# A wider list schedule for the tail of a fused attention, gated-expert and cosine MLP kernel

## The chip, the cores and the metric

The kernel runs on one core of a Trainium2 chip. A core has five engines that take their instructions in program order, each from its own queue, and meet at semaphores: TensorE (PE in the profile, with its weight loads as PEld), VectorE (DVE), ScalarE (ACT), GpSimd (POOL) and SyncE (SP, which here issues most of the DMAs). The metric is the device time of one launch in microseconds (us).

## The reference

```python
def _attn_ref(q, k, v):                    # (2, 8, 576, 64)
    scores = scale * np.matmul(q, k.transpose(0, 1, 3, 2))
    mask = (rel >= 0) & (rel < 64)
    attn = softmax(np.where(mask, scores, -1e9))
    return np.matmul(attn, v)

def _moe_ref(x, domain_probs, w1, w2):     # x (1152, 512), 4 experts 512 -> 1024 -> 512
    p = domain_probs / (domain_probs.sum(-1, keepdims=True) + 1e-09)
    for e in range(E):
        h = np.maximum(x @ w1[e], 0.0)
        out += p[:, e:e + 1] * (h @ w2[e])

def _moe2_ref(x, w_in, w_out):             # 512 -> 2048 -> 512
    h = x @ w_in
    g = h * np.cos(h)
    return g @ w_out
```

The three run one behind the other on the same 1152 tokens.

## The kernel before

Every product of float32 numbers is made as three matmuls of rounded parts (high by high, low by high, high by low), so each tile that enters a product exists as a high part (`xhi`, `thi`, `whi`, `w7hi`, `hh`), which ACT makes, and a low part (`xlo`, `tlo`, `wlo`, `w7lo`, `hl`), which DVE or POOL makes as the difference. PE adds the three products up in a PSUM bank.

The program has two parts. The **hand-written part** holds the attention and the first steps of the gated experts, in the order of the string `ORDER`. The gated experts are cut into eight halves e of an expert; a step (e, g, f) treats one group g of token columns with one block f of hidden columns. Its A step (L431 to L433, or L628 in the scheduled part) makes the hidden block, L444 its high and L447 its low part; its B step (L469) adds the block's share into the PSUM accumulators `pb_acc` of the group, and behind the last f one `add_expert` for each accumulator (L478 for the first half, L480 for the others, on DVE) adds it, times the gate, to `acc` in SBUF and so frees the bank. There are four such accumulator banks. The line `for what, s in seq[:T2 + 1]` emits the steps that are written by hand; with T2 = 30 the last of them are B(1,1,0), B(1,1,1) and A(0,2,0).

All that follows is the **scheduled part**: the code makes a list of jobs (`job`, `either` for a job that DVE or POOL may take), each with an engine, a duration from a formula, what it depends on, and the PSUM banks or buffers that it takes or uses (`Slots`, `Hold`). It holds the rest of the first two halves (L628, L469), the seven-product units of the other halves (`a_unit`, `b_unit`), and the cosine MLP. In `a_unit` PE makes products `y` and `seed` from `xhi`, `thi` and the weights `w7` (L1037); ACT copies a `seed` (L1051) or a product `p` (L1055) back into PSUM or SBUF, DVE adds (L1068 `y`, L1077 `c`), and the finished sum goes through ACT and DVE into `hh` and `hl` (L444 and L1130 for the experts; for the cosine MLP `kk` through L1146, L1151, L1157, L1158 and L1163, then `hh` L1166 and `hl` L1172). `b_unit` adds them up in PSUM (L1231 `pb_acc`), and L480 or L1256 takes them out. Beside it run: sums of weights (`sums` L850) with their parts (L869, L874, L913, L918), sums of token columns (`tsum` L944, L953, parts L966, L969), the change of the last weights from 64-bit words (`m`, `x`: L737 to L770 on DVE and POOL), and, between the experts and the cosine MLP, `turn` and `token_sums`, which transpose `acc` on PE (`psx` L1303) and make new `xhi` (L1318), `xlo` (L1328) and `tsum` (L1371 to L1403) of it.

The planner `plan` plays the jobs through. A job's due time `late` is worked out backwards from the PE jobs in their order. PE takes its jobs in the order of `pe_list`, with leave to look eight ahead; another engine that is free takes, of the jobs that are ready, the one with the earliest due time. `plan` runs three times, each time with the starts of the last one, and the instructions of all engines are then written out in the order of the planned starts. On the chip nothing is reordered any more: an instruction whose data is late holds up what stands behind it on its engine.

One detail matters for the adds: `std_bs` makes the `Hold` on the accumulators only at f = 0. For the half (1,1), whose f = 0 step is hand-written, `std_finish` finds no `Hold`, so the planner does not know that the adds of (1,1) free the banks that the B step of (0,2) wants.

Of the kernel before, what the change touches and what calls it, by code (L numbers as in the profile page):

```python
# [26 lines left out]
def tile_window_attention_moe_cosglu(  # L27
# [20 lines left out]
    NE, DM, FF = w1.shape  # L48
# [3 lines left out]
    NFC = FE // P  # L52
    SPL = FF // FE
# [477 lines left out]

    T2 = 2 * SPL * 2 * NFC - 2
    for what, s in seq[:T2 + 1]:
# [43 lines left out]
    def dve_ns(n):  # L577
        return 77 + 1.01 * n
# [69 lines left out]
    def std_bs(s):  # L648
        e, g, f = steps[s]
        no = GS[g] // P  # L650
        deps = [std_ready.get(s), std_b.get(s - 1)]
        if f == 0:
            std_hold[e, g] = [Hold(accs) for _ in range(no)]
        holds = std_hold.get((e, g), ())

        def matmuls():
            emit_b(s)

        b = std_b[s] = pe(
            no * 3 * mm_ns(DM), matmuls, deps,  # L660
            new=holds if f == 0 else (), use=holds if f else (),
        )
        return b
# [3 lines left out]
    def std_finish(e, g, b):  # L667
        k, c = SG[g], GC[g] // P
        for i in range(GS[g] // P):
            def add(i=i):  # L670
                p = gate_p[:, G0[g] // P + i, e // SPL:e // SPL + 1]
                add_expert(e, acc[k][:, c + i, :], std_pss[e, g][i], p)
            hold = std_hold.get((e, g))
            std_done[k, c + i] = job(
                "DVE", dve_ns(DM), add, [b], use=[hold[i]] if hold else ()
            )

# [789 lines left out]
    POOLMAX = 9999  # L1467
    QUIET = 1
    SOON = 60000.0
    place = {j: i for i, j in enumerate(pe_list)}  # L1470
# [24 lines left out]

    def plan(starts):
        line = list(pe_list)
# [43 lines left out]
        engines = ["PE", "ACT", "DVE", "POOL", "SP", None]  # L1541
        waiting = {e: [] for e in engines}

        def arrive(j):
# [10 lines left out]
        while events:  # L1555
# [59 lines left out]
        return began  # L1615

    rank = {j: i for i, j in enumerate(topo)}
# [59 lines left out]
```

## Time and profile before

| | |
|---|---|
| median of three runs | 638.83 us (637.6 to 639.07) |
| the profiled execution, its own time | 639.75 us |
| its span, from the first to the last instruction | 637.8 us |
| outside the span | 1.95 us |
| PE busy | 622.8 us, 98% of the span |
| DVE busy | 470.6 us, 74% |
| ACT busy | 335.2 us, 53% |
| POOL busy | 156.9 us, 25% |

The time of the profiled execution is 0.92 us above the median. A stretch's busy times tell which engine is full there, the granted clock which of PE's two levels it had (1.00 is 2.4 GHz, 0.50 is 1.2 GHz), and the timeline which instruction PE waited for: a row's bracket holds the idle time ahead of the instruction and the instruction that ended it.

### The profile page before, as it was taken

What the parts mean: (1) busy time and instruction counts of PE and PEld (TensorE: products, weight loads), DVE (VectorE), ACT (ScalarE), POOL (GpSimd) and SP (SyncE); (2) the same over time, 40 slices, a digit from 0 to 9 for tenths busy, and PEclk for the clock granted to TensorE, in tenths of its full rate; (3) what the DMA queues carried; (4) which work ended last, traced back from release to release, by engine and by line L of the source; (5) the groups of instructions that cost most, each with busy time, mean ns of one, the idle gap of its engine ahead of it and who ended that gap; (6) DMA issues with size and microseconds to landing.
All of it is one profiled execution on the core that took longest, in us unless ns stands there. A gap on an engine that the chain in (4) does not pass through costs nothing.

```text
span 637.8 us, 10837 instructions
## 1 busy us (share of the span) xinstructions
PE 622.8 (98%) x4019; PEld 553.2 (87%) x4019; DVE 470.6 (74%) x990; ACT 335.2 (53%) x840; POOL 156.9 (25%) x169
## 2 busy tenths in 40 slices
PE   8999999899999999999999999999899999999997
PEld 7878898688888989989999988998799988999896
DVE  5858536544999799889789699787857677676664
ACT  5957313232345244335344244457878978777653
POOL 6985101230022110223333220212114124121000
PEclk9999999899999999999999999999899999999999
DMA  9943200260055444444446645204001202000022
GB/s 299 294 149 105 69 1 29 71 197 1 1 166 163 135 131 133 166 133 166 137 130 208 186 132 166 68 0 133 2 1 58 76 7 93 2 1 1 1 67 83
DMA packets 37254, 63.10 MB, mean 99 GB/s; under 512 B 2761, under 2 KB 18633, under 8 KB 37202
## 3 DMA queue, kind: packets, MB, share of 16 engines
q1 hardware_dynamic: 36386, 61.63, 30.8%
q10 hardware_dynamic: 816, 0.79, 0.4%
q8 instruction: 31, 0.51, 0.4%
q14 instruction: 21, 0.17, 0.1%
HBM read 51.66 MB, written 10.75 MB: 98 GB/s over the span
## 4 chain that ended last, share of the span: by engine, by line
PE 85%; DVE 7%; ACT 3%; DMA 2%; issue 1%; POOL 1%; DVEq 0%; SPq 0%; POOLq 0%
PE pb_acc L1231 37%; PE y L1037 19%; PE seed L1037 14%; PE pb_acc L469 7%; PE ph L628 2%; ACT e L284 1%; PE ph L431 1%; PE ph L433 1%; PE ph L432 1%; DMA raw<-in_moe_w_dram 1%; PE psv L324 1%; DVE acc L480 1%; PE pss L260 1%; PE pst L309 1%; DVE tsum L944 1%
## 5 line engine op out<-in xcount | busy, mean ns | idle before, releaser
L1231 PE MATMUL pb_acc<-whi,hh 128*128 128x512 f32 x360 | 142.1, 395 | 2.3 <-DVE xlo L1328 2.3
L1231 PE MATMUL pb_acc<-wlo,hh 128*128 128x512 f32 x360 | 142.1, 395 | 0.0
L1231 PE MATMUL pb_acc<-whi,hl 128*128 128x512 f32 x360 | 140.8, 391 | 0.0
L1037 PE MATMUL y<-xhi,w7hi 128*128 128x256 f32 (+1 forms) x320 | 95.3, 298 | 0.8 <-DVE hl L1172 0.5
L1037 PE MATMUL y<-xhi,w7lo 128*128 128x256 f32 (+1 forms) x320 | 94.7, 296 | 0.0
L1037 PE MATMUL y<-xlo,w7hi 128*128 128x256 f32 (+1 forms) x320 | 94.7, 296 | 0.0
L1231 PEld LDWEIGHTS pb_acc<-whi,hl 128*128 128x128 f32 x360 | 67.9, 189 | 15.5
L1231 PEld LDWEIGHTS pb_acc<-whi,hh 128*128 128x128 f32 x360 | 67.9, 189 | 12.0 <-issue 2.5
L1231 PEld LDWEIGHTS pb_acc<-wlo,hh 128*128 128x128 f32 x360 | 67.9, 189 | 8.7
L1037 PE MATMUL seed<-thi,w7hi 128*128 128x320 f32 (+1 forms) x240 | 71.4, 298 | 2.0 <-DVE y L1068 1.0
L1037 PE MATMUL seed<-thi,w7lo 128*128 128x320 f32 (+1 forms) x240 | 70.7, 295 | 0.0
L1037 PE MATMUL seed<-tlo,w7hi 128*128 128x320 f32 (+1 forms) x240 | 70.6, 294 | 0.0
L1037 PEld LDWEIGHTS y<-xhi,w7hi 128*128 128x128 f32 x320 | 60.6, 189 | 3.1 <-DVE hl L1172 0.7
L1037 PEld LDWEIGHTS y<-xlo,w7hi 128*128 128x128 f32 x320 | 60.6, 189 | 1.8
L1037 PEld LDWEIGHTS y<-xhi,w7lo 128*128 128x128 f32 x320 | 60.4, 189 | 0.0
L874 POOL TENSOR_TENSOR w7lo<-raw,w7hi 128x256 fp32r<-128x256 f32 (+1 forms) x21 | 17.9, 856 | 139.0 <-DVE sums L850 50.3
L1037 PEld LDWEIGHTS seed<-thi,w7hi 128*128 128x128 f32 x240 | 45.1, 188 | 7.5 <-DVE y L1068 1.2
L480 DVE SCALAR_TENSOR_TENSOR acc<-pb_acc,gate_p,acc 128x512 f32<-128x512 f32 x63 | 46.1, 744 | 6.3 <-PE pb_acc L1231 6.3
L1037 PEld LDWEIGHTS seed<-tlo,w7hi 128*128 128x128 f32 x240 | 45.1, 188 | 3.8
L444 ACT ACTIVATE hh<-y 128x320 fp32r<-128x320 f32 (+1 forms) x48 | 19.5, 407 | 50.2 <-PE y L1037 50.1
L918 POOL TENSOR_TENSOR wlo<-raw,whi 128x512 fp32r<-128x512 f32 x20 | 26.4, 1328 | 78.5 <-ACT whi L913 43.8
L1037 PEld LDWEIGHTS seed<-thi,w7lo 128*128 128x128 f32 x240 | 45.1, 188 | 0.0
(141 smaller groups left out, 1323.7 us busy)
## 6 DMA issues: line engine op xcount, KB each, us to landing
raw<-in_moe_w_dram SPq DMA_DIRECT2D x32, 512.0 KB, 5.2
raw<-in_moe_w_in_dram SPq DMA_DIRECT2D x16, 512.0 KB, 4.3
w<-x SPq DMA_DIRECT2D x32, 256.0 KB, 4.7
raw<-in_moe_w_out_dram SPq DMA_DIRECT2D x16, 512.0 KB, 4.4
raw<-w SPq DMA_DIRECT2D x16, 512.0 KB, 3.4
vr<-in_v_dram SPq DMA_DIRECT2D x16, 256.0 KB, 4.3
out_dram<-acc SPq DMA_DIRECT2D x18, 128.0 KB, 1.7
qraw<-in_q_dram SPq DMA_DIRECT2D x16, 128.0 KB, 3.7
```

The costliest lines, as they stand in the source:

```text
L260: nc.tensor.matmul(out=out[h][W * c:W * (c + 1), p], lhsT=qts[c][rows, p, :], rhs=kts[c][rows, p, :], start=True, stop=True,)
L284: nc.scalar.activation(out=e[:, p], in_=s[:, p], func=AF.Exp, bias=nm[:, p:p + 1], scale=1.0, accum_out=sm[:, p:p + 1],)
L309: nc.tensor.transpose(out=ps[:, p], in_=pn[:, p], identity=ident)
L324: nc.tensor.matmul(out=pv[W * h:W * (h + 1), p, W * c:W * (c + 1)], lhsT=vts[c][:, P * p + W * h:P * p + W * (h + 1)], rhs=pts[h][:, p, W ...
L444: nc.scalar.activation(out=hh, in_=ps, func=AF.Relu)
L469: nc.tensor.matmul(out=ps, lhsT=a, rhs=b, start=first and m == 0, stop=last and m == 2)
L480: nc.vector.scalar_tensor_tensor(out=a, in0=ps, scalar=p, in1=a, op0=ALU.mult, op1=ALU.add)
L628: nc.tensor.matmul(out=ps, lhsT=a[:, d, cs], rhs=b[:, d, :], start=d == 0 and m == 0, stop=d == KD - 1 and m == 2,)
L874: return engine.tensor_tensor(out=operand(w_lo[x], i), in0=part(i), in1=operand(w_hi[x], i).bitcast(F32), op=ALU.subtract,)
L918: return engine.tensor_tensor(out=w_lo[x][:, i], in0=box["t"][:, i], in1=w_hi[x][:, i].bitcast(F32), op=ALU.subtract,)
L1037: nc.tensor.matmul(out=ps, lhsT=a[:, WI[i], d, :], rhs=b[:, d, :], start=start and d == 0 and m == 0, stop=d == 1 and m == 2, skip_group_c ...
L1231: nc.tensor.matmul(out=ps, lhsT=a, rhs=b[:, fo, :], start=first and fo == 0 and m == 0, stop=last and fo == 1 and m == 2,)
```

## The change

Three steps of the gated experts, B(1,1,0), B(1,1,1) and A(0,2,0), go from the hand-written part to the scheduler (T2 is lower by three). Holds on the accumulators are made for every group, so that the adds of (1,1) count as what frees the banks. In `plan` a job that takes several slots starts only when so many are free; DVE, ACT and POOL leave a job that is ready if a more urgent one is to arrive before it would end (`waits_better`); and due times get a random addition of up to 0, 300 or 1000 ns. In place of three passes there are 120 plans; each is played back in its written order with random delays (`rehearse`), and the best one is written out.

```diff
-    T2 = 2 * SPL * 2 * NFC - 2
+    T2 = 2 * SPL * 2 * NFC - 5
...
         deps = [std_ready.get(s), std_b.get(s - 1)]
-        if f == 0:
+        begun = (e, g) in std_hold
+        if not begun:
             std_hold[e, g] = [Hold(accs) for _ in range(no)]
-        holds = std_hold.get((e, g), ())
+        holds = std_hold[e, g]
+        if f and not begun:
+            job(None, 0.0, lambda: None, new=holds)
...
-            hold = std_hold.get((e, g))
-            std_done[k, c + i] = job(
-                "DVE", dve_ns(DM), add, [b], use=[hold[i]] if hold else ()
-            )
+            std_done[k, c + i] = job("DVE", dve_ns(DM), add, [b], use=[std_hold[e, g][i]])
...
+    PLANS = 120
...
-    def plan(starts):
+    def plan(starts, jitter):
...
+        open_ = {j: len(j.deps) for j in jobs}
+        coming = {e: {} for e in engines}
+        soon = {j: 0.0 for j in jobs}
+
+        def waits_better(j, e, ns):
+            end = now + ns
+            return any(
+                now < at < end and u.late < end and j.late > at + u.ns
+                for x in (("DVE",) if e == "POOL" else (e,)) for u, at in coming[x].items()
+                if e == x or u.port
+            )
...
-                            free[h.slots] > (e == "SP" or e == "PE" and j is not todo[0])
+                            free[h.slots] >= len(j.new) + (e == "SP" or e == "PE" and j is not todo[0])
                             for h in j.new
...
+                    if e in ("DVE", "ACT", "POOL"):
+                        ns = {"DVE": dve_ns, "POOL": pool_ns}.get(e)
+                        ok = [j for j in ok if not waits_better(j, e, ns(j.size) if j.size else j.ns)]
                     if not ok:
                         break
-                    j = ok[0] if e == "PE" else min(ok, key=lambda j: (j.late, j.n))
+                    j = ok[0] if e == "PE" else min(ok, key=lambda j: (j.late + jitter[j], j.n))
...
+                    coming[e].pop(j, None)
+                    for o in j.out:
+                        open_[o] -= 1
+                        soon[o] = max(soon[o], now + j.ns + gap(j, o))
+                        if not open_[o] and not o.size and o.eng != "PE":
+                            coming[o.eng][o] = soon[o]
...
+    def rehearse(starts, seed):
+
+        draw = random.Random(seed)
+        line = sorted(jobs, key=lambda j: (starts[j], rank[j]))
...
+                for o in j.out:
+                    left[o] -= 1
+                    late = draw.uniform(-SPARE, 0.0) if j.eng == "SP" else 0.0
+                    at[o] = max(at[o], now + gap(j, o) + late)
...
+                    ns = j.ns * (1.0 if e == "PE" else 1.0 + abs(draw.gauss(0.0, 0.02)))
+                    busy[e] = now + ns
...
+        return last if len(ended) == len(jobs) else 1e9
...
-    for _ in range(3):
-        began = plan(began)
+    best, asked = None, began
+    for n in range(PLANS):
+        if n % 4 == 0:
+            draw = random.Random(n)
+            spread = (0.0, 300.0, 1000.0)[n // 4 % 3]
+            jitter = {j: draw.uniform(0.0, spread) for j in jobs}
+        try:
+            asked = plan(asked, jitter)
+        except AssertionError:
+            asked = began
+            continue
+        end = sum(rehearse(asked, seed) for seed in range(3))
+        if best is None or end < best[0]:
+            best = end, asked, [(j.eng, j.ns, j.tail) for j in jobs]
+    began = best[1]
+    for j, kept in zip(jobs, best[2]):
+        j.eng, j.ns, j.tail = kept
```

The counts of instructions of PE, ACT and SP are the same in both programs. Twelve more of the jobs that either engine may do lie on DVE and as many fewer on POOL. PE's order is the same up to its first cosine units behind 455 us. What moves stands on the other engines; line numbers of the kernel after are higher by one in the places below.

On DVE, at the end of the first two halves (the hand-written part ends here), before; `hl` is the low part of an A step, L480 the last add of (1,1), its first two stand three rows further up:

```order
L447 SCALAR_TENSOR_TENSOR hl<-ph,hh 128x512
L944 TENSOR_TENSOR tsum<-xhi,xlo 128x128
L850 TENSOR_TENSOR sums<-raw 128x256
L953 TENSOR_TENSOR tsum<-tsum 128x128
L850 TENSOR_TENSOR sums<-raw,sums 128x256
L874 TENSOR_TENSOR w7lo<-raw,w7hi 128x512
L969 TENSOR_TENSOR tlo<-tsum,thi 128x6x64
L447 SCALAR_TENSOR_TENSOR hl<-ph,hh 128x512
L969 TENSOR_TENSOR xlo<-tsum,xhi 128x2x64
L874 TENSOR_TENSOR w7lo<-sums,w7hi 128x512
L850 TENSOR_TENSOR sums<-raw,sums 128x256
L480 SCALAR_TENSOR_TENSOR acc<-pb_acc,gate_p,acc 128x512
```

The same place after:

```order
L875 TENSOR_TENSOR w7lo<-raw,w7hi 128x512
L851 TENSOR_TENSOR sums<-raw,sums 128x256
L970 TENSOR_TENSOR xlo<-tsum,xhi 128x2x64
L970 TENSOR_TENSOR tlo<-tsum,thi 128x6x64
L970 TENSOR_TENSOR xlo<-tsum,xhi 128x2x128
L875 TENSOR_TENSOR w7lo<-sums,w7hi 128x512
L448 SCALAR_TENSOR_TENSOR hl<-ph,hh 128x512
L851 TENSOR_TENSOR sums<-raw,sums 128x256
L481 SCALAR_TENSOR_TENSOR acc<-pb_acc,gate_p,acc 128x512 x3
L448 SCALAR_TENSOR_TENSOR hl<-ph,hh 128x512 x2
L851 TENSOR_TENSOR sums<-raw 128x256 x2
L851 TENSOR_TENSOR sums<-raw,sums 128x256
```

The three adds of (1,1) now stand together (the row with x3), ahead of the two L448 and the three `sums` that follow them here; before, the third stood alone at the end of twelve rows.

On DVE, in the first seven-product unit behind the standard steps, before (`x` is the change from 64-bit words, L1068 and L1077 the two adds for which PE waits, L480 an add that frees a bank):

```order
L480 SCALAR_TENSOR_TENSOR acc<-pb_acc,gate_p,acc 128x512
L850 TENSOR_TENSOR sums<-raw 128x256
L765 TENSOR_TENSOR x_2071<-x_2071,m_2070 128x512
L850 TENSOR_TENSOR sums<-raw,sums 128x256
L770 SCALAR_TENSOR_TENSOR x_2071<-raw_1986,x_2071 128x512
L1068 TENSOR_TENSOR y_2166<-seed,p_2182 128x256
L874 TENSOR_TENSOR w7lo<-sums,w7hi 128x512
L1130 SCALAR_TENSOR_TENSOR hl<-y_2156,hh 128x256
L850 TENSOR_TENSOR sums<-raw,sums 128x256
L1077 TENSOR_TENSOR c_2215<-seed,p_2182 128x256
L770 SCALAR_TENSOR_TENSOR x_2058<-raw_1983,x_2058 128x512
L480 SCALAR_TENSOR_TENSOR acc<-pb_acc,gate_p,acc 128x512
```

After:

```order
L851 TENSOR_TENSOR sums<-raw 128x256
L481 SCALAR_TENSOR_TENSOR acc<-pb_acc,gate_p,acc 128x512
L851 TENSOR_TENSOR sums<-raw 128x256
L760 SCALAR_TENSOR_TENSOR x_2071<-raw_1986,x_2071 128x512
L1069 TENSOR_TENSOR y_2169<-seed,p_2185 128x256
L481 SCALAR_TENSOR_TENSOR acc<-pb_acc,gate_p,acc 128x512
L1078 TENSOR_TENSOR c_2213<-seed,p_2185 128x256
L1131 SCALAR_TENSOR_TENSOR hl<-y_2159,hh 128x256
L875 TENSOR_TENSOR w7lo<-sums,w7hi 128x512
```

From the add of an accumulator (L480 at the top, L481 in the second row after) to the unit's L1068 (L1069) there were four instructions between, now there are two; the next add, six rows below L1068 before, follows it directly.

On DVE, where the experts end and the cosine MLP begins, before (`psx` is a transposed block of `acc`, L1328 takes it out of its bank; `y_5056` is the product whose bank comes next):

```order
L1077 TENSOR_TENSOR c_5130<-seed_5064,p_5087 128x256
L1151 SCALAR_TENSOR_TENSOR kk<-kk,y_5042 128x256
L1378 SCALAR_TENSOR_TENSOR tsum<-psx,tsum 128x128 x2
L1151 SCALAR_TENSOR_TENSOR kk<-kk,c_5130 128x256
L1151 SCALAR_TENSOR_TENSOR kk<-kk,y_5056 128x256
L1387 TENSOR_TENSOR tsum<-tsum 128x128 x3
L1163 TENSOR_TENSOR y_5042<-y_5042,kk 128x256
L1387 TENSOR_TENSOR tsum<-tsum 128x128 x3
L1163 TENSOR_TENSOR y_5056<-y_5056,kk 128x256
L1387 TENSOR_TENSOR tsum<-tsum 128x128 x2
L1328 SCALAR_TENSOR_TENSOR xlo<-psx,xhi 128x2x128
L1163 TENSOR_TENSOR c_5130<-c_5130,kk 128x256
```

After (its name is `y_5048` here):

```order
L1078 TENSOR_TENSOR c_5122<-seed_5058,p_5079 128x256
L1152 SCALAR_TENSOR_TENSOR kk<-kk,y_5033 128x256
L1379 SCALAR_TENSOR_TENSOR tsum<-psx,tsum 128x128
L1329 SCALAR_TENSOR_TENSOR xlo<-psx,xhi 128x2x128
L1152 SCALAR_TENSOR_TENSOR kk<-kk,c_5122 128x256
L1152 SCALAR_TENSOR_TENSOR kk<-kk,y_5048 128x256
L1388 TENSOR_TENSOR tsum<-tsum 128x128
L1379 SCALAR_TENSOR_TENSOR tsum<-psx,tsum 128x128
L1164 TENSOR_TENSOR y_5033<-y_5033,kk 128x256
L1379 SCALAR_TENSOR_TENSOR tsum<-psx,tsum 128x128
L1388 TENSOR_TENSOR tsum<-tsum 128x128
L1379 SCALAR_TENSOR_TENSOR tsum<-psx,tsum 128x128
```

The instruction that empties the bank of `psx` has gone up from the tenth row behind L1077 to the third behind L1078, ahead of all sums L1388. The product of `y_5048` with its cosine (L1164) and its low part (L1173) follow further down.

## Rows read from the trace of the kernel before

**Rows 1.** Busy time, share of the span and instruction count of each engine, from the page
```profile
PE 622.8 (98%) x4019; PEld 553.2 (87%) x4019; DVE 470.6 (74%) x990; ACT 335.2 (53%) x840; POOL 156.9 (25%) x169
```

**Rows 2.** Stretches: length, then each engine's busy time (instructions), clock share, DMA share, GB/s
```profile
117.61:121.02 3.41, 3.41 (x9) 2.63 (x9) 1.33 (x3) 0.54 (x2) 2.27 (x4) 0.50 0.82 281
121.02:179.00 57.98, 57.98 (x294) 50.08 (x294) 33.54 (x66) 16.88 (x34) 7.13 (x6) 1.00 0.17 56
179.00:184.00 5.00, 3.71 (x28) 3.17 (x27) 5.00 (x13) 3.03 (x8) 1.28 (x1) 1.00 0.56 141
184.00:440.00 256.00, 255.91 (x1518) 230.69 (x1517) 222.13 (x439) 111.13 (x245) 57.17 (x54) 1.00 0.46 143
455.53:458.94 3.41, 3.41 (x11) 2.87 (x10) 3.41 (x11) 2.42 (x7) 0.00 (x0) 0.50 0.02 5
459.00:634.00 175.00, 175.00 (x1004) 157.04 (x1003) 114.45 (x255) 125.75 (x294) 33.91 (x32) 1.00 0.10 32
```

**Rows 3.** Timeline, PE at 114 to 118.5: start, duration, instruction, [idle before <-releaser]
```profile
117.39 0.63 PE L469 MATMUL pb_acc<-whi,hh 128*128 128x512 f32 x1 [2.92 <-DVE acc L480]
```

**Rows 4.** Timeline, DVE at 93 to 121
```profile
100.50 0.69 DVE L447 SCALAR_TENSOR_TENSOR hl<-ph,hh 128x512 fp32r<-128x512 f32 x1 [6.45 <-ACT hh L444]
101.11 1.42 DVE L944 TENSOR_TENSOR tsum<-xhi,xlo 128x256 f32<-128x256 f32 x4
102.45 0.76 DVE L953 TENSOR_TENSOR tsum<-tsum 128x256 f32<-128x256 f32 x2
...
109.18 0.95 DVE L969 TENSOR_TENSOR tlo<-tsum,thi 128x768 fp32r<-128x768 f32 x1
...
110.25 1.40 DVE L480 SCALAR_TENSOR_TENSOR acc<-pb_acc,gate_p,acc 128x512 f32<-128x512 f32 x2
...
116.59 0.74 DVE L480 SCALAR_TENSOR_TENSOR acc<-pb_acc,gate_p,acc 128x512 f32<-128x512 f32 x1
```

**Rows 5.** Timeline, PE at 179 to 183.6
```profile
180.44 0.38 PE L1037 MATMUL seed<-thi,w7hi 128*128 128x256 f32 x1 [1.01 <-DVE y L1068]
...
183.29 0.39 PE L1037 MATMUL y<-xhi,w7hi 128*128 128x256 f32 x1 [0.28 <-DVE acc L480]
```

**Rows 6.** Timeline, DVE at 168 to 184
```profile
168.42 0.48 DVE L1130 SCALAR_TENSOR_TENSOR hl<-seed,hh 128x320 fp32r<-128x320 f32 x1
...
170.09 0.42 DVE L753 TENSOR_SCALAR x<-m 128x512 uint32<-128x512 uint32 x1
170.42 0.42 DVE L953 TENSOR_TENSOR tsum<-tsum 128x256 f32<-128x256 f32 x1
...
178.42 0.69 DVE L765 TENSOR_TENSOR x<-x,m 128x512 f32<-128x512 f32 x1
179.02 0.42 DVE L850 TENSOR_TENSOR sums<-raw,sums 128x256 f32<-128x256 f32 x1
...
179.96 0.43 DVE L1068 TENSOR_TENSOR y<-seed,p 128x256 f32<-128x256 f32 x1
```

**Rows 7.** Timeline, PE at 443.5 to 459
```profile
445.02 0.39 PE L1037 MATMUL y<-xhi,w7hi 128*128 128x256 f32 x1 [0.51 <-DVE hl L1172]
...
447.30 0.38 PE L1037 MATMUL seed<-thi,w7hi 128*128 128x256 f32 x1 [0.86 <-ACT seed L1051]
...
455.26 0.52 PE L1231 MATMUL pb_acc<-whi,hh 128*128 128x512 f32 x1 [2.30 <-DVE xlo L1328]
...
457.71 0.47 PE L1037 MATMUL y<-xhi,w7hi 128*128 128x320 f32 x1
```

**Rows 8.** Timeline, DVE at 440 to 460
```profile
450.49 0.41 DVE L1077 TENSOR_TENSOR c<-seed,p 128x256 f32<-128x256 f32 x1
...
454.70 0.41 DVE L1328 SCALAR_TENSOR_TENSOR xlo<-psx,xhi 128x256 fp32r<-128x256 f32 x1
```

**Rows 9.** Timeline, ACT at 440 to 460
```profile
454.08 0.51 ACT L1158 ACTIVATE kk<-kk,bias_h 128x256 f32<-128x256 f32 x1
454.49 0.36 ACT L1166 ACTIVATE hh<-y 128x256 fp32r<-128x256 f32 x1
```

More of the change, by code (lines that the diff above doesn't have):

```diff
@@ L1 @@
 import heapq
+import random
 from contextlib import ExitStack
@@ L1615, in plan @@
         return began
+    def rehearse(starts, seed):
+        draw = random.Random(seed)
+        line = sorted(jobs, key=lambda j: (starts[j], rank[j]))
+        queues, turns, behind, held, users = {}, {}, {}, {j: [] for j in jobs}, {}
+        previous = None
+        for j in line:
+            queues.setdefault(j.eng, []).append(j)
+            if j.eng == "POOL":
+                behind[j] = previous
+            elif j.port:
+                previous = j
+            for h in j.new:
+                turns.setdefault(h.slots, []).append(h)
+                users[h] = len(h.users)
+                for u in h.users:
+                    held[u].append(h)
+        free = {s: s.free for s in turns}
+        left = {j: len(j.deps) for j in jobs}
+        at = dict.fromkeys(jobs, 0.0)
+        busy = dict.fromkeys(queues, 0.0)
+        nth = dict.fromkeys(queues, 0)
+        events, seen, port, owner, ended, last = [(0.0, 0, None)], 0, 0.0, "POOL", set(), 0.0
+        while events:
+            now = events[0][0]
+            while events and events[0][0] <= now + 1e-6:
+                j = heapq.heappop(events)[2]
+                if j is None:
+                    continue
+                ended.add(j)
+                last = now
+                for h in held[j]:
+                    users[h] -= 1
+                    free[h.slots] += not users[h]
+                for o in j.out:
+                    left[o] -= 1
+                    late = draw.uniform(-SPARE, 0.0) if j.eng == "SP" else 0.0
+                    at[o] = max(at[o], now + gap(j, o) + late)
+                    if not left[o]:
+                        seen += 1
+                        heapq.heappush(events, (max(at[o], now), seen, None))
+            more = True
+            while more:
+                more = False
+                for e in ("PE", "ACT", *(("POOL", "DVE") if owner == "DVE" else ("DVE", "POOL")), "SP", None):
+                    if nth[e] == len(queues[e]) or busy[e] > now + 1e-6:
+                        continue
+                    j = queues[e][nth[e]]
+                    if left[j] or at[j] > now + 1e-6 or j.port and port > now + 1e-6:
+                        continue
+                    if behind.get(j) and behind[j] not in ended or any(
+                        free[h.slots] < len(j.new) or h not in turns[h.slots][:len(j.new)] for h in j.new
+                    ):
+                        continue
+                    for h in j.new:
+                        free[h.slots] -= 1
+                        turns[h.slots].remove(h)
+                    nth[e] += 1
+                    ns = j.ns * (1.0 if e == "PE" else 1.0 + abs(draw.gauss(0.0, 0.02)))
+                    busy[e] = now + ns
+                    if j.port:
+                        port, owner = busy[e], e
+                    for done in (j, None):
+                        seen += 1
+                        heapq.heappush(events, (now + ns, seen, done))
+                    more = True
+        return last if len(ended) == len(jobs) else 1e9
@@ L1622, in tile_window_attention_moe_cosglu @@
         t += j.ns
-    for _ in range(3):
-        began = plan(began)
+    best, asked = None, began
[8 more added lines that the diff above has]
+            asked = began
+            continue
+        end = sum(rehearse(asked, seed) for seed in range(3))
[4 more added lines that the diff above has]
+        j.eng, j.ns, j.tail = kept
     ahead = None
```

## The prediction

> **What bounds the kernel now.** I read the page's busy line first, then a table of stretches, then the timeline of PE inside the stretches where PE is not full, and last the engines that its brackets name. PE is busy 622.8 of 637.8 us, 98% [rows 1], so only what makes PE wait, or runs it at its lower clock, can be won. The table says where that is: from 121 to 179, from 184 to 440 and from 459 to 634 us PE's busy time equals the length of the stretch to 0.1 us, at clock 1.00 [rows 2]. No order of the other engines can gain anything there; it can only lose. The start (hand-written, not touched) and the 3.8 us behind the last matmul stay as they are. What is left lies at three places.
>
> Place A, the end of the first two halves. PE waits 2.92 us ahead of the 512-wide L469 at 117.39, released by an L480 add [rows 3]. That add is the third of (1,1); the two before it ran at 110.25, it ran only at 116.59 [rows 4]. Behind the wait, from 117.61 to 121.02, the granted clock is 0.50, PE's level of 1.2 GHz [rows 2]: 3.41 us in which half of the time is lost, 1.7 us. Place A costs 2.92 + 1.7 = 4.6 us.
>
> Place B, the first seven-product unit. PE waits 1.01 us for an L1068 and 0.28 us for an L480 [rows 5], while DVE is busy for the whole of 179 to 184 [rows 2]. The clock is 1.00 there and behind it. 1.3 us.
>
> Place C, from the experts to the cosine MLP. Waits of 0.51, 0.86 and 2.30 us, the last for the L1328 that empties a `psx` bank [rows 7], and again a stretch of 3.41 us at clock 0.50 [rows 2], 1.7 us. 5.4 us.
>
> The three hold 4.6 + 1.3 + 5.4 = 11.3 us. That is the most that the change can bring.
>
> **The change part by part.** The planning itself happens before the program exists and costs no device time. The matmuls, the ACT work and the DMAs are the same in number; what moves is order, and twelve jobs from POOL to DVE.
>
> A, the adds. Before, DVE stood idle for 6.45 us ahead of the L447 at 100.50 and began its 128x256 `tsum` work only behind it [rows 4], since that L447 was the last hand-written instruction. After, the `tsum` work stands ahead of it and can start at 100.50 - 6.45 = 94.05. Up to the three adds DVE then has 21 instructions of 256 columns, 7 of 128, 4 of 512, 2 of 768 and one of 384. Four of 256 take 102.45 - 101.11 = 1.34, so 0.335 each [rows 4]; 512 columns take 179.02 - 178.42 = 0.60 [rows 6]; 768 take at most 0.95 [rows 4]; I take 0.2 for 128 and 0.5 for 384, about in proportion. Sum: 7.0 + 1.4 + 2.4 + 1.9 + 0.5 = 13.2, so the adds begin at about 107.3, and at 0.74 at most each [rows 4] the third ends at 109.5. Some of the 35 instructions wait for parts that ACT and POOL make of the sums; with 2 us for that it is 111.5. The B step whose result they read is over by 110.25, when the first of them ran before; from there it would be 112.5. PE wants the bank at 117.39 - 2.92 = 114.47 [rows 3]. Margin 2 to 5 us: the wait goes. What was late next there, the other L447 of these steps, stands earlier or just behind the adds. Without the wait PE is full there, and I expect no lower clock. Gain 4.6; bounds 2.9 (clock falls all the same) and 4.6.
>
> B, the add of the unit. Between the start of the L1130 at 168.42 and of L1068 at 179.96 DVE spent 11.54 us [rows 6]. After, the instructions between the same two are: nine of 256 columns and two L754 at 0.335 each (L753 took 170.42 - 170.09 = 0.33 [rows 6]), the L1131 itself at 0.4, five more of the word change at 0.60, four L481 at 0.70 (two took 1.40 [rows 4]) and one of 768 at 0.9: 3.7 + 0.4 + 3.0 + 2.8 + 0.9 = 10.8 us. L1069 begins at 179.2, 0.75 earlier, which leaves some 0.2 of the 1.01. The next add follows it directly and ends by 180.4, long before PE's want at 183.0: the 0.28 goes. Gain 0.8 + 0.3 = 1.1, bounds 0 and 1.3. The work that moved behind (L765, two `sums`, L770) has its readers later in the unit, where the order puts it ahead of them.
>
> C, the bank of `psx`. L1329 now stands third behind L1078, which began at 450.49 before [rows 8]; so it runs at about 451.5 in place of 454.70, and PE, which wants the bank at 455.26 - 2.30 = 452.96 [rows 7], does not wait. But a new wait takes its place. Six 512-wide L1231 later PE comes to the first `y` of the next unit, which took its turn at 457.71 [rows 7]; its bank is that of `y_5048`, and this is free when `y_5048`'s low part is made. On ACT the last of the three cosine chains ends, as before, near 454.5 [rows 9]. Before, the high part of this product came first behind it (0.36); after, another one comes ahead of it, so 454.5 + 2 x 0.36 = 455.2, and the low part on DVE (0.41, as other work of 256 columns there [rows 8]) ends at 455.6; if ACT's chains start a little earlier, 455.2. I take 455.4. The six took 457.71 - 455.26 = 2.45 us, nearly all of it at half clock; at full clock I take 1.3, and PE would be there at 454.3, so it waits about 1.1. The two smaller waits ahead stay: the 0.51 shrinks to some 0.2 since the low part that it waits for has one product (L1164) fewer ahead of it, the 0.86 grows to some 1.2 since the seed copy has another weight cast (L870) ahead of it on ACT. So the `y` starts at 455.4 and not at 457.71: 2.3; and the rest of the slow stretch behind it, 458.94 - 457.71 = 1.2, costs no half any more: 0.6. Gain 2.9; if the clock falls again, 2.9 - 1.7 = 1.2; bounds 0 and 5.4.
>
> Here a page bears on the clock. The rows show that three waits of 0.51, 0.86 and 2.30 at C were followed by clock 0.50, two of 1.01 and 0.28 at B were not [rows 2, 5, 7]. After, C has about 0.2, 1.2 and 1.1, in sum between the two. The Trainium skill, "TensorE: Matmul & The Clock Gate", section "A second HAM failure mode: psum-queue depth-cycling", says that short idle times between groups of matmuls, from waiting for PSUM, can be enough to let the clock fall and rise. By that C would keep its slow stretch and the time would be 1.7 higher than my sum. B in this trace speaks against it, A and C for it.
>
> The twelve jobs. DVE takes about twelve of 0.335 to 0.60 us more, some 4.6 us, over stretches where it is busy 222 of 256 us [rows 2]. On average that fits, but DVE is full in places. No row shows a new wait, so bounds: nothing, or one wait like those of B with a slow stretch as at A, 1.3 + 1.7 = 3.0. I take 0.5, near the lower end, because PE had no wait at all in 256 us with DVE 87% full.
>
> Sum: 639.75 - 4.6 - 1.1 - 2.9 + 0.5 = 631.65 for an execution like the profiled one. That one lay 0.92 above the median, so 630.7 for the median.
>
> **The rivals.** First, the clock falls again at C: 630.7 + 1.7 = 632.4. For it: three waits still stand close together. Against it: their sum is 2.5 where it was 3.67, and B's two changed nothing.
>
> Second, the loss moves into the stretches that are full now. DVE's added work and the new order make L1068 or L480 late in some of the expert units between 184 and 440. One such place costs up to 3.0 (above), and by that 631 to 637 for one or two. It becomes slower than before with four: 630.2 + 4 x 3.0 = 642.2; the point is 640.75 - 630.2 = 10.5 us, three and a half such places. For it: DVE is full at B, and L1068 stands behind work of no hurry. Against it: PE never waits in 256 us before, and the look-ahead keeps long jobs from starting just ahead of urgent ones.
>
> Third, the change does not do at A what it says: the parts that DVE needs ahead of the adds come so late from ACT and POOL that the third add still ends behind 114.47. That takes 5 us of waits among 35 instructions. Then only B and C are won, 638.83 - 1.1 - 2.9 + 0.5 = 635.3, and if C is lost to new waits too, 638: no difference.
>
> **How the numbers follow.** Forecast, A and B gone, C partly, clock kept (627.5 to 632): 0.55. Clock falls at C (632 to 633.5): 0.17. One or two new places, or A only in part (633.5 to 636.9): 0.14. No difference, within 0.3% (636.9 to 640.7; about what a measurement of this kernel can tell from no change): 0.07. Slower: 0.07. Faster is the first three, 0.86. The range runs from 627.5, where all 11.3 us are won, to 635.3, the third rival's time; it leaves out about 0.19.
>
> **What would show it.** In the profile after, PE has no wait for the L481 of (1,1) near 114 us and clock 1.00 through 110 to 125; the L1037 that waited for L1068 near 175 (all is some 5 us earlier by then) has at most 0.2 us ahead of it; near 448 PE waits about 1 us for an L1173 and not 2.3 for an L1329; 184 to 440 has no idle time. Wrong would be: a slow stretch behind C, any wait over 0.5 us on L1069 or L481 in the expert units, or a third add of (1,1) later than 114.

## The result, and the profile after

The kernel after takes 630.74 us in the median of four runs (630.69 to 631.07), the kernel before 638.81 beside it (637.6 to 639.07). The ratio is 0.9878, with a 95% interval of 0.9861 to 0.9895: faster by 8.1 us, 1.3%. The profiled execution of the kernel after took 630.69 us with a span of 628.9; the one before 639.75 and 637.8. From profile to profile that is 9.06 us, 1.0 more than between the medians.

The busy line and the clock line of the page after, which answer to [rows 1]:

```profile
PE 620.4 (99%) x4019; PEld 551.0 (88%) x4019; DVE 477.9 (76%) x1002; ACT 337.0 (54%) x840; POOL 146.9 (23%) x157
PEclk9999999999999999999999999999999999999999
```

The granted clock has no dip any more; before it had two. DVE is busy 7.3 us longer than before and POOL 10 us shorter. PE's busy time is 2.4 us lower although the matmuls are the same: the two slow stretches had added 3.4 us, while PE is 0.7 us busier in the first 100 us (97.36 for 96.70) and 0.5 us busier in the expert units.

The stretches of the kernel after, which answer to [rows 2] (length, busy time of PE, PEld, DVE, ACT, POOL with instructions, clock share, DMA share, GB/s):

```profile
110.00:121.00 11.00, 11.00 (x49) 8.96 (x49) 5.66 (x7) 4.13 (x9) 4.43 (x5) 1.00 0.32 106
173.50:178.00 4.50, 4.44 (x37) 4.23 (x35) 3.99 (x10) 2.53 (x8) 1.98 (x2) 1.00 0.09 36
178.00:437.00 259.00, 258.92 (x1529) 232.63 (x1528) 231.21 (x461) 113.39 (x250) 42.50 (x36) 1.00 0.45 138
439.97:450.00 10.03, 8.06 (x52) 7.02 (x52) 9.92 (x37) 9.68 (x30) 2.27 (x2) 1.00 0.33 105
450.00:455.00 5.00, 5.00 (x29) 4.48 (x28) 4.99 (x14) 4.85 (x12) 1.72 (x2) 1.00 0.01 3
```

Place A lies in the first of them: PE is full and the clock is 1.00. Place B is the second: 4.44 of 4.50. The long stretch of expert units is full to 0.08 us, as before. Place C, 439.97 to 450, still has 1.97 us of idle time, and the clock behind it is 1.00.

PE's timeline after at the three places, which answers to [rows 3], [rows 5] and [rows 7]:

```profile
114.22 0.39 PE L470 MATMUL pb_acc<-whi,hh 128*128 128x512 f32 x1
```

```profile
174.59 0.39 PE L1038 MATMUL seed<-thi,w7hi 128*128 128x256 f32 x1
...
176.91 0.28 PE L1038 MATMUL y<-xhi,w7hi 128*128 128x256 f32 x1
```

```profile
438.56 0.38 PE L1038 MATMUL y<-xhi,w7hi 128*128 128x256 f32 x1
...
440.86 0.38 PE L1038 MATMUL seed<-thi,w7hi 128*128 128x256 f32 x1 [0.88 <-ACT seed L1052]
...
446.57 0.40 PE L1232 MATMUL pb_acc<-whi,hh 128*128 128x512 f32 x1
...
449.21 0.41 PE L1038 MATMUL y<-xhi,w7hi 128*128 128x320 f32 x1 [1.09 <-DVE hl L1173]
```

The first row is the L470 that waited 2.92 us before; it has no bracket now. The same matmul as at 180.44 before stands at 174.59, the one at 183.29 stands at 176.91, neither with a bracket. At C the four rows are the ones at 445.02, 447.30, 455.26 and 457.71 before: the first and third have lost their brackets, the second keeps 0.88 us, and the fourth has a new one of 1.09 us, released by the L1173 that makes a low part.

Where the 8.9 us of span come from is read from the lead of the kernel after, the difference between the starts of the same matmul in both traces. These are the last matmul ahead of A's wait, the last ahead of B's first wait and the second behind B's second, the last ahead of C's first wait and the first at full clock behind C, before and then after (the row at 180.66 is for the paragraph behind):

```profile
114.08 0.39 PE L469 MATMUL pb_acc<-whi,hl 128*128 128x512 f32 x1
...
179.16 0.28 PE L1037 MATMUL y<-xhi,w7lo 128*128 128x256 f32 x1
...
180.66 0.28 PE L1037 MATMUL seed<-tlo,w7hi 128*128 128x256 f32 x1
...
183.52 0.28 PE L1037 MATMUL y<-xlo,w7hi 128*128 128x256 f32 x1
...
444.23 0.28 PE L1037 MATMUL y<-xhi,w7lo 128*128 128x256 f32 x1
...
459.01 0.31 PE L1037 MATMUL y<-xhi,w7lo 128*128 128x320 f32 x1
```

```profile
113.99 0.39 PE L470 MATMUL pb_acc<-whi,hl 128*128 128x512 f32 x1
...
174.26 0.28 PE L1038 MATMUL y<-xhi,w7lo 128*128 128x256 f32 x1
...
177.02 0.28 PE L1038 MATMUL y<-xlo,w7hi 128*128 128x256 f32 x1
...
438.25 0.28 PE L1038 MATMUL y<-xhi,w7lo 128*128 128x256 f32 x1
...
450.05 0.31 PE L1038 MATMUL y<-xhi,w7lo 128*128 128x320 f32 x1
```

The lead is 0.09 us ahead of A, 4.90 ahead of B, 6.50 behind B, 5.98 ahead of C and 8.96 behind C; at the end it is 8.9. So A gave 4.8, B 1.6 and C 3.0, and 0.5 was lost in the 260 us of expert units.

B gave more than the brackets hold, 1.01 and 0.28. A bracket begins at the modelled end of the matmul ahead, 0.28 us behind its start, while matmuls of 256 columns otherwise start 0.12 apart; and the one behind a wait is followed after 0.22 in place of 0.12. From 179.16 by way of 180.44 to 180.66 PE took 1.50 us for two steps that otherwise take 0.24: the wait cost 1.26 where its bracket says 1.01.

### The profile page after: what moved, and what is told of

It is laid out like the page before. It is cut to its first block, busy times and chain, and to the rows that moved or that the text cites. A ratio compares the mean times of both kernels' runs of the same rounds, so it can differ in the third digit from the quotient of the medians.

```text
span 628.9 us, 10809 instructions
## 1 busy us (share of the span) xinstructions
PE 620.4 (99%) x4019; PEld 551.0 (88%) x4019; DVE 477.9 (76%) x1002; ACT 337.0 (54%) x840; POOL 146.9 (23%) x157
## 4 chain that ended last, share of the span: by engine, by line
PE 81%; DVE 11%; DMA 3%; ACT 2%; issue 2%; POOL 1%; ACTq 0%; DVEq 0%; SPq 0%; POOLq 0%
PE pb_acc L1232 33%; PE y L1038 17%; PE seed L1038 13%; PE pb_acc L470 8%; PE ph L629 4%; PE psv L325 1%; PE ph L432 1%; PE ph L433 1%; PE ph L434 1%; DMA raw<-in_moe_w_dram 1%; DVE acc L481 1%; PE pst L310 1%; PE pss L261 1%; DVE x L766 1%; DVE m L744 1%
## 5 line engine op out<-in xcount | busy, mean ns | idle before, releaser
L1232 PE MATMUL pb_acc<-whi,hh 128*128 128x512 f32 x360 | 141.7, 394 | 0.0
L1232 PE MATMUL pb_acc<-wlo,hh 128*128 128x512 f32 x360 | 141.6, 393 | 0.0
L1232 PE MATMUL pb_acc<-whi,hl 128*128 128x512 f32 x360 | 140.4, 390 | 0.0
L1232 PEld LDWEIGHTS pb_acc<-whi,hl 128*128 128x128 f32 x360 | 67.6, 188 | 15.5
L1232 PEld LDWEIGHTS pb_acc<-whi,hh 128*128 128x128 f32 x360 | 67.7, 188 | 9.4
L1232 PEld LDWEIGHTS pb_acc<-wlo,hh 128*128 128x128 f32 x360 | 67.8, 188 | 8.7
L919 POOL TENSOR_TENSOR wlo<-raw,whi 128x512 fp32r<-128x512 f32 x22 | 29.1, 1333 | 114.4 <-ACT whi L914 48.5
L481 DVE SCALAR_TENSOR_TENSOR acc<-pb_acc,gate_p,acc 128x512 f32<-128x512 f32 x63 | 46.0, 746 | 5.7 <-PE pb_acc L1232 5.6
L875 POOL TENSOR_TENSOR w7lo<-raw,w7hi 128x256 fp32r<-128x256 f32 (+1 forms) x18 | 16.6, 926 | 117.4 <-DVE sums L851 49.3
L870 ACT CAST w7hi<-sums 128x512 fp32r<-128x512 f32 x40 | 24.8, 622 | 27.4 <-DVE sums L851 24.8
```

The costliest lines, as they stand in the source:

```text
L481: nc.vector.scalar_tensor_tensor(out=a, in0=ps, scalar=p, in1=a, op0=ALU.mult, op1=ALU.add)
L870: nc.scalar.copy(out=operand(w_hi[x], i), in_=part(i))
L875: return engine.tensor_tensor(out=operand(w_lo[x], i), in0=part(i), in1=operand(w_hi[x], i).bitcast(F32), op=ALU.subtract,)
L919: return engine.tensor_tensor(out=w_lo[x][:, i], in0=box["t"][:, i], in1=w_hi[x][:, i].bitcast(F32), op=ALU.subtract,)
L1232: nc.tensor.matmul(out=ps, lhsT=a, rhs=b[:, fo, :], start=first and fo == 0 and m == 0, stop=last and fo == 1 and m == 2,)
```

## Place A: each of three parts removes it alone

First run: the three steps go to the scheduler, nothing else.

```diff
-    T2 = 2 * SPL * 2 * NFC - 2
+    T2 = 2 * SPL * 2 * NFC - 5
```

> The kernel before, with the three steps given to the scheduler and nothing else; three passes of the old planner. The order at places B and C is the same as before, the three adds of (1,1) stand together ahead of the second sums with w7lo. Theory (place A is a matter of order at the seam): the wait of 2.92 us and the slow stretch at A go, B (1.3 us) and C (3.67 us and a slow stretch) stay word for word: 638.8 - 4.6 = 634.2. Rival 1 (it takes the look-ahead and the 120 plans): A stays, 638.8. Rival 2 (the clock falls at A for another reason than the wait): only 2.9 is won, 635.9.

Measured: 634.74 us (632.8 to 634.95), ratio 0.9917 (0.9894 to 0.9940). Waits of PE in its profile (who waited for whom: sum, times, longest, in us), and its stretches at A, at C and behind C:

```profile
PE pb_acc L1231 <- DVE xlo L1328: 2.3, 1, 2.3
...
PE seed L1037 <- DVE y L1068: 1.0, 1, 1.0
PE seed L1037 <- ACT seed L1051: 0.9, 1, 0.9
PE y L1037 <- DVE hl L1172: 0.5, 1, 0.5
```

```profile
110.00:121.00 11.00, 11.00 (x49) 9.01 (x48) 5.16 (x8) 4.89 (x10) 4.74 (x5) 1.00 0.32 115
438.50:450.00 11.50, 7.83 (x57) 6.95 (x56) 11.40 (x41) 10.37 (x32) 1.29 (x1) 1.00 0.00 1
450.00:456.00 6.00, 6.00 (x32) 5.22 (x33) 5.03 (x16) 4.56 (x12) 1.30 (x1) 1.00 0.01 3
```

A is gone with PE full and the clock up; B and C have the waits of before to 0.02 us. The theory holds and rival 1 falls; rival 2 falls in this execution, where the clock at A is 1.00 once the wait is gone. What was not expected stands in the last row: C's waits are those of before and the clock behind them is 1.00 in this execution. The other three had a mean clock of 0.996 and took 1.9 to 2.2 us longer; no profile shows where their clock fell. This is taken up below.

Second run: the holds alone, the three steps still written by hand.

```diff
-        if f == 0:
+        begun = (e, g) in std_hold
+        if not begun:
             std_hold[e, g] = [Hold(accs) for _ in range(no)]
-        holds = std_hold.get((e, g), ())
+        holds = std_hold[e, g]
+        if f and not begun:
+            job(None, 0.0, lambda: None, new=holds)
```

> The kernel before, with the holds on accumulators made for every half and nothing else; the three steps stay hand-written, so DVE begins its tsum work at 100.5 us as before. The adds of (1,1) stand behind the second L447, some 17 rows earlier than the third add did. Theory (the planner did not know that the adds free banks): the adds run by 111 us, ahead of PE's want at 114.5, A goes, B and C stay: 634.2. Rival (it is the late start of DVE's tsum work that made the adds late, and the holds alone do not help): A stays in part, 636 to 638.8.

Measured: 633.63 us (632.46 to 634.97), ratio 0.9913 (0.9887 to 0.9940). Its DVE at A:

```profile
100.36 1.42 DVE L944 TENSOR_TENSOR tsum<-xhi,xlo 128x256 f32<-128x256 f32 x4
...
107.80 2.05 DVE L480 SCALAR_TENSOR_TENSOR acc<-pb_acc,gate_p,acc 128x512 f32<-128x512 f32 x3
```

DVE begins its `tsum` work as late as before (100.36, before 101.11), and the three adds run at 107.80 all the same, because the planner puts them ahead of the rest of that work. PE has no wait at A. So the late start of the `tsum` work was not what made the third add late; its place in DVE's queue was.

Third run: the planner alone. The three steps are hand-written again and the holds are as before; look-ahead, jitter, playback and 120 plans stay.

```diff
-    T2 = 2 * SPL * 2 * NFC - 5
+    T2 = 2 * SPL * 2 * NFC - 2
...
-        begun = (e, g) in std_hold
-        if not begun:
+        if f == 0:
             std_hold[e, g] = [Hold(accs) for _ in range(no)]
```

> The kernel after, with the three steps hand-written again and the holds as before: only look-ahead, jitter, playback and 120 plans are left. The adds of (1,1) stand together behind the tsum work, the add of the first unit has one L771 and one sums between it and the L481, the L1329 at C stands behind five L1388. Theory (each of the three parts is enough at A; the planner does B and C): A, B gone, about 2.5 won at C, 0.5 lost in the full stretches: 630.9 to 631.5. Rival (holds or T2 are needed at A): 635.5 and a wait at A.

Measured: 631.56 us (631.07 to 631.62), ratio 0.9872 (0.9854 to 0.9891). All waits of its PE over 0.3 us behind the start:

```profile
PE seed L1038 <- ACT seed L1052: 1.3, 1, 1.3
...
PE seed L1038 <- DVE y L1069: 0.9, 2, 0.5
```

That is just above the 630.9 to 631.5 that were expected, and the rival's wait at A did not come. The interval overlaps with that of the whole change. So the planner alone is worth what the whole change is, within what these runs can tell, and at A the three parts do the same work three times.

## Place C and the clock

One instruction of the kernel before is moved by hand: the L1328 that empties the `psx` bank, to right behind the first L1151 of that place.

```diff
+    lows = sorted(
+        (j for j in jobs if j.eng == "DVE" and "turn.<locals>.low" in j.fn.__qualname__), key=lambda j: began[j]
+    )
+    began[lows[7]] = max(began[d] + d.ns for d in lows[7].deps) + 1900
     ahead = None
```

> The kernel before with one instruction moved by hand: the L1328 that empties the psx bank at C stands right behind the first L1151 there, ten rows earlier. Theory (place C as predicted: the 2.30 us go, a wait of about 1.1 us for the low part of y follows, the clock keeps its level): 638.8 - 2.8 = 636.0, and clock 1.00 behind C. Rival 1 (the clock falls again, since three waits of 0.5, 0.9 and 1.1 stand close together): 637.7. Rival 2 (the y product's bank was as late as the psx bank, so the wait only changes its name): 638.8.

Measured: 637.58 us (635.53 to 639.58, seven runs) against 639.38, ratio 0.9971 (0.9952 to 0.9991). Waits of PE, then its stretches behind A, at C and behind C:

```profile
PE pb_acc L469 <- DVE acc L480: 2.9, 1, 2.9
PE y L1037 <- DVE hl L1172: 1.8, 2, 1.3
PE seed L1037 <- ACT seed L1051: 1.1, 2, 0.9
```

```profile
117.08:120.49 3.41, 3.41 (x9) 2.63 (x8) 1.24 (x3) 0.45 (x2) 2.34 (x3) 0.50 0.81 277
444.00:456.00 12.00, 9.33 (x63) 8.01 (x62) 11.93 (x42) 10.99 (x34) 1.29 (x1) 1.00 0.00 1
456.00:462.00 6.00, 5.75 (x32) 4.87 (x32) 4.60 (x14) 4.32 (x11) 1.30 (x1) 1.00 0.01 3
```

The 2.3 us have become 1.26 us for a low part, as the prediction has it for the kernel after (1.8 in two waits, of which 0.5 were there before), so rival 2 falls. A keeps its wait and its slow stretch; behind C the clock is 1.00 in this execution, against rival 1. But the time is rival 1's 637.7 and not the theory's 636.0: the theory took 638.8 for the kernel before, which took 639.38 here, and PE, counted from start to start, gained 2.0 us at C in place of 2.8, since a new wait of 0.25 us for the next seed copy took back 0.5.

The seven times spread over 4 us: one execution has mean clock 1.000 (635.53), five 0.997 (636.85 to 637.98), one 0.994 (639.58). By these clocks one kernel had none, one or two falls of the clock. If the single fall lies at A in all of them, as in the profile, A's wait of 2.92 us was followed by one in six of seven. Where the second fall of the execution at 0.994 lies was not seen; it can be at C, behind the shorter waits.

The same edit with the three steps in the scheduler, so that A does not disturb:

> The kernel before with the three steps given to the scheduler and the one L1328 at C moved up; no holds, look-ahead or playback. With the three steps alone C kept its waits of 0.5, 0.9 and 2.3 us; in one execution the clock stayed at 1.00 behind them (632.8), in three others the mean clock was 0.996 and the time 634.7 to 635.0. Theory (the fall of the clock hangs on the last wait): with 0.5, 0.9 and 1.3 it stays up in every execution, 632.8 - 2.3 + 1.3 = 631.8, all within 0.5. Rival (the clock falls at C by chance whatever the last wait is): the times fall into two groups again, 631.8 and 633.8.

Measured: 632.66 us, four runs within 632.55 and 632.9, all with mean clock 0.999 or 1.000. The theory holds in what it said of the clock. Four executions do not rule the rival out: at the rate of 5 in 11 that is counted below, four of four without a fall come by chance in one case of eleven, and these ran on another chip. The time is 0.9 above what was expected. Between the two profiles, of 632.8 and 632.55 us, PE gained 1.0 at the shorter wait, a new wait of 0.27 us behind it took back 0.5 from start to start, and the hand-written start was 0.3 slower.

The next run asks where a fall lies in an execution with the old waits at C: it is the kernel with the three steps alone again, on a third chip.

> The same kernel as in the run with the three steps alone, for another profile: in its profiled execution the clock stayed up (632.8), in its three other executions the mean clock was 0.996 and the time 634.7 to 635.0, and only the profile shows where. Theory (the fall belongs to the 2.3 us wait at C): a slow stretch begins right behind the L1231 that waits for L1328, near 450 us, and the execution takes about 634.8. Rival (it falls somewhere else, at A or in the start): the slow stretch stands elsewhere. If the clock stays up again, this stays open.

Measured: 632.96 to 633.65, mean clock 0.999 in all three, no fall. The place stays unseen in this kernel; that it is C rests on the profile of before, whose second slow stretch begins 0.3 us behind the start of the matmul that had waited 2.30 us, and is not shown for these executions.

Counted over all runs without a wait at A: with the old waits at C (0.5, 0.9 and 2.3 us) the mean clock was 0.996 in 5 of 11 executions, and those took about 2 us more than their neighbours. Of the 28 executions of the seven kernels whose longest wait behind the start was 1.6 us or less (the one with both edits, the kernel after, the planner alone, and four of the next section) none had a mean clock under 0.999. The kernel with only C moved is not among them, because of A's wait.

## The planner: picking among plans

Three kernels change only which plan is written out. The kernel's own playback gives an end for each plan: 531.8 for the chosen one of 120, counted from the first scheduled step.

```diff
-    PLANS = 120
+    PLANS = 3
```

> The kernel after with 3 plans in place of 120, so that the best of the first three is kept; all else the same. The kernel's own playback ends 3.5 us later for it (535.4 against 531.8). Theory (the playback tells what the chip does): 630.7 + 3.5 = 634.2. Rival (plans differ on paper alone, waits on the chip come from what no plan knows): 630.7 to 631.5.

Measured: 634.47 us (634.09 to 635.69), ratio 0.9924 (0.9907 to 0.9940); span 632.3, that is 3.4 over the kernel after, where the playback had 3.6.

```diff
-        if best is None or end < best[0]:
+        if end < 1e8 and (best is None or end > best[0]):
```

> The kernel after, but of its 120 plans the one that ends last in the playback is written out (541.4 against 531.8). Theory (playback ranks plans rightly): 630.7 + 9.5 = 640.2, and more if the clock falls. Rival (plans differ on paper alone): under 633.

Measured: 643.46 us (642.78 to 644.25), ratio 1.0062 (1.0045 to 1.0078): slower than before, with the same jobs. The two waits of PE ahead of its first slow stretch, and its two slow stretches:

```profile
376.30 0.38 PE L1038 MATMUL y<-xhi,w7hi 128*128 128x256 f32 x1 [0.82 <-DVE hl L1131]
...
378.21 0.58 PE L1038 MATMUL seed<-thi,w7hi 128*128 128x256 f32 x1 [0.93 <-DVE y L1069]
```

```profile
378.15:381.56 3.41, 2.93 (x12) 2.63 (x12) 2.29 (x6) 0.39 (x2) 0.00 (x0) 0.50 0.92 354
460.07:463.48 3.41, 3.41 (x11) 2.82 (x10) 3.41 (x12) 2.20 (x6) 0.00 (x0) 0.50 0.02 5
```

The span is 13.6 over the kernel after; without the half of 2 x 3.41 it is 10.2, where the playback had 9.6. The first fall comes behind waits of 0.82 and 0.93 us, 2 us apart, so here a fall did not need one long wait; the second comes behind a wait of 1.76 us, while a wait of 1.60 at 382.74 was followed by none. Two of the four executions have a mean clock of 0.994, the others 0.996 and 0.997.

```diff
-    PLANS = 120
+    PLANS = 240
```

> The kernel after with 240 plans in place of 120; the best one ends at 530.9 in the playback in place of 531.8. Theory: 630.7 - 0.9 = 629.8. Rival (what is left are waits that the playback does not see, some 0.5 us): no difference, 630.4 to 631.2.

Measured: 630.58 us (630.39 to 631.38), ratio 0.9863 (0.9846 to 0.9880). No difference from the kernel after that can be told. Its longest wait:

```profile
PE seed L1038 <- ACT seed L1052: 1.6, 1, 1.6
```

The 0.9 us that the playback promised did not come: 1.6 us at the seed copy of C is more than the kernel after has in its longest wait. Between plans the playback's differences of 3.6 and 9.6 us came true on the chip; its difference of 0.9 did not.

The last two runs, both on one further chip, take out what makes the plans differ: look-ahead, and then jitter too.

```diff
-                    if e in ("DVE", "ACT", "POOL"):
-                        ns = {"DVE": dve_ns, "POOL": pool_ns}.get(e)
-                        ok = [j for j in ok if not waits_better(j, e, ns(j.size) if j.size else j.ns)]
```

> The kernel after without look-ahead; jitter, playback and 120 plans are left. Playback 531.8, the same as of the kernel after. Theory (picking does it): 630.7 to 631.3. Rival (look-ahead is needed): 632.5 or more, with waits on L1069 or L1173 behind long jobs of no hurry.

Measured: 631.28 us (630.81 to 631.71), ratio 0.9894 (0.9876 to 0.9911).

```diff
-            spread = (0.0, 300.0, 1000.0)[n // 4 % 3]
+            spread = (0.0, 0.0, 0.0)[n // 4 % 3]
```

> The kernel after without look-ahead and without jitter on due times: 120 passes of the planner, each from the starts of the last, and the best by playback. Playback 532.2 against 531.8 of the kernel after and 534.4 of three passes of the old planner (measured 632.8 with the clock up). Theory (the gain at B and C comes from picking among many plans, whatever makes them differ): 630.7 + 0.4 = 631.1, clock 1.00. Rival (look-ahead is needed, as the prediction put it against its second rival): waits like those of the third plan, 632.5 or more.

Measured: 631.44 us (631.13 to 631.55), ratio 0.9896 (0.9881 to 0.9911). Both lie 0.5 to 0.7 above the kernel after, with intervals that overlap with its own. So look-ahead and jitter are worth some half a microsecond here, if that, and repeating the planner and keeping the best is worth 3.7 (3 plans against 120).

What the repeats buy is not place B. PE's wait for the L1069 there, with 3 plans and then with 120 but without look-ahead:

```profile
174.32 0.39 PE L1038 MATMUL seed<-thi,w7hi 128*128 128x256 f32 x1 [0.39 <-DVE y L1069]
```

```profile
175.22 0.38 PE L1038 MATMUL seed<-thi,w7hi 128*128 128x256 f32 x1 [0.72 <-DVE y L1069]
```

Even the worst plan has 0.38 there, and the plans without look-ahead or jitter 0.71, where the wait was 1.01 before. So in these profiles B hardly depends on the number of plans: without look-ahead some 0.7 us stay, with it 0.4 or less. With 3 plans the loss lies at C (1.29 and 1.47 us) and in three waits of 0.55 to 0.72 that the kernel after does not have. No run takes out by itself the rule that a job starts only when as many slots are free as it takes.

## Why the prediction was right, and where it was not

The forecast of 630.7 met 630.74, and the mechanism was right; that the two agree to 0.04 us is luck. For an execution like the profiled one the sum had 631.65, 8.1 less than before; the profiled execution of the kernel after took 630.69, 9.06 less. The gain was 0.9 to 1.0 larger than the sum, half of it at B. This was made up by the last step, which took off the 0.92 us by which the profiled execution before lay above its median. That excess did not carry over: the profiled execution after lies at its median. Why the other executions before took less is open, as their clocks are not on record. The steps, one by one:

- What bounds the kernel: right. Nothing was gained outside the three places, and the order cost a little inside the full stretches.
- A, 4.6: the wait and the slow stretch went, as forecast; by the leads A gave 4.8. The three adds began at 107.88 and ended at 109.95, against 107.3 and 109.5 worked out:

```profile
107.88 2.07 DVE L481 SCALAR_TENSOR_TENSOR acc<-pb_acc,gate_p,acc 128x512 f32<-128x512 f32 x3
```

  The working was right for the kernel after; the reason given for it, the earlier start of the `tsum` work, was not the needed one, as the run with the holds alone shows.
- B, 1.1: from the start of the L1131 to the L1069 took 10.59 us, where 10.8 was worked out, and the next add follows directly:

```profile
163.51 0.48 DVE L1131 SCALAR_TENSOR_TENSOR hl<-seed,hh 128x320 fp32r<-128x320 f32 x1
...
174.10 0.44 DVE L1069 TENSOR_TENSOR y<-seed,p 128x256 f32<-128x256 f32 x1
174.44 0.76 DVE L481 SCALAR_TENSOR_TENSOR acc<-pb_acc,gate_p,acc 128x512 f32<-128x512 f32 x1
```

  PE's matmul at 174.59 starts 0.33 behind the one ahead of it, which is 0.2 more than the usual distance of 0.12, as forecast. The order was right, but the term was too small: by the leads B gave 1.6, since a wait costs more than its bracket.
- C, 2.9: the L1329 runs long ahead of PE's want at 446.57, and the new wait for a low part is 1.09 us, where 1.1 was forecast. The order on ACT and DVE is the one that the sum used, two high parts and then the low part:

```profile
448.07 0.64 ACT L1167 ACTIVATE hh<-y 128x256 fp32r<-128x256 f32 x2
```

```profile
444.98 0.41 DVE L1329 SCALAR_TENSOR_TENSOR xlo<-psx,xhi 128x256 fp32r<-128x256 f32 x1
...
448.74 0.42 DVE L1173 SCALAR_TENSOR_TENSOR hl<-y,hh 128x256 fp32r<-128x256 f32 x1
```

  Of the smaller waits one went (0.51, forecast 0.2) and one stayed at 0.88 (forecast 1.2). The lead grew by 3.0 at C, so this term was 0.1 off.
- The twelve jobs on DVE, 0.5: 0.5 was lost between 178 and 437 us, at two places. Some 0.2 lies near 324 us: PE's order differs there from that before, which the front of this document overlooked; two tiles of L1232 went ahead of a `seed`, and the lead falls from 6.43 to 6.25. Some 0.3 lies at 359.58, where PE's weight load for a `seed` waits for an L1069 (DVE, PEld):

```profile
357.84 0.69 DVE L760 SCALAR_TENSOR_TENSOR x<-raw,x 128x512 f32<-128x512 uint32 x1
358.45 0.74 DVE L481 SCALAR_TENSOR_TENSOR acc<-pb_acc,gate_p,acc 128x512 f32<-128x512 f32 x1
359.11 0.42 DVE L1069 TENSOR_TENSOR y<-seed,p 128x256 f32<-128x256 f32 x1
...
359.58 0.19 PEld L1038 LDWEIGHTS seed<-thi,w7hi 128*128 128x128 f32 x1 [0.50 <-DVE y L1069]
```

  The L1069 stands behind four jobs of the word change (from 356.05 on, the L760 is the last) and an add. Before, the same matmul stood at 365.61 and the L1068 had run at 363.80, 1.8 us ahead of it. So the loss is of the kind that the prediction named; whether these jobs are among the twelve is not shown.
- The rivals: the clock did not fall again at C in four executions, A did what it should, and of the second rival only the small wait at 359.58 came. Against that rival the prediction set the look-ahead; without it the time is 0.5 higher and the expert units have no more than a wait of 0.43 us, so that argument carried little.

Another size was off without showing in the total. Both slow stretches were counted as fixed terms of 1.7 us. They are chances: a fall came in 6 of 7 executions of the kernel with only C moved, which has A's wait, and in 5 of 11 of the kernels with C's old waits and none at A, there at about 2 us. On the page named in the prediction, the Trainium skill, "TensorE: Matmul & The Clock Gate", section "A second HAM failure mode: psum-queue depth-cycling", short idle times of PE from cycling through PSUM banks can make the clock fall and rise. The worst plan agrees (0.82 and 0.93 us for banks that DVE freed, then clock 0.50), while the kernel after, with 0.88 and 1.09 us 8 us apart, kept its clock in four executions of four. The prediction was right to hold it for a rival and to keep it under one in five; it took B's pair of waits as evidence from a single execution, which was too little.

## What to carry to other kernels

Where a hand-written part hands over to a planner, look at what the planner does not know there: an add that frees a bank had a late due time because its bank was not counted, and it sat 5 us too long in a queue that was never reordered. Picking by playback was worth more here than a cleverer rule: 120 repeats without look-ahead and jitter, the best kept, came within 0.7 us of the kernel after, and 3 plans with both stayed 3.7 behind it. And where one engine is full, price a wait by the starts of the matmuls around it, not by its bracket alone, add the chance that the clock falls behind it, and judge kernels by several executions, since the chance alone moved one kernel by 2 to 4 us.

## What the runs showed of the hardware that was not expected

The clock's fall is not fixed by the program: the kernel with the three steps alone took 632.8 us with mean clock 0.999 and 634.7 to 635.0 with 0.996, and 632.96 to 633.65 without a fall on another chip. Its waits are known from two profiles, both without a fall; those of the longer executions were not seen. The kernel before shows the same: in 28 executions beside these runs it had mean clocks of 0.992 to 0.997 and took 636.96 to 641.37 us. Each of the five slow stretches that the profiles of three kernels show in mid-program lasted 3.41 us; the 2 us by which executions with a mean clock of 0.996 are longer are more than the half of that, and no profile of such an execution shows why. That stays open.
